# A gated MLP and a linear attention on one core: operands of the spatial products at equal addresses modulo 256

## The chip, the cores and the metric

The kernel runs on one core of a Trainium2 chip. The core has TensorE (PE), VectorE (DVE), ScalarE (ACT), GpSimd (POOL) and SyncE (SP), an on-chip memory of 128 partitions, and accumulators (PSUM) that TensorE writes. A matmul takes a left operand, which is loaded as weights (the profile's PEld), and a right operand, which streams past them. An *address* below is the byte offset of an operand in its partition. The metric is the time of one execution in device microseconds, the median of some runs.

## The reference

Two branches work on a layer-normed x and are added to it: a linear attention with learned features (A), and a gated MLP (B). The change is in the spatial product of B, where a 2048 x 2048 matrix multiplies 2048 x 688 activations:

```python
xn = _layernorm(x, axis=-1)                       # x: 1 x 2048 x 512
z = _gelu(jnp.einsum("bsd,df->bsf", x, w_in))     # here x is xn, F = 1376
z1 = z[..., :Fh]                                  # Fh = 688
z2 = _layernorm(z[..., Fh:], axis=-1)
g = jnp.einsum("ts,bsf->btf", w_sp, z2) + b_sp[None, :, None]
return jnp.einsum("bsf,fd->bsd", z1 * g, w_out)
...
return x + _A_ref(xn, ...) + _B_ref(xn, ...)
```

## The kernel before

All matrix products run in three matmuls each (`mm3`, L55): a number is split into a rounded high part and a rest (`b_parts`, L592: ACT rounds, DVE subtracts), and high x high, high x rest and rest x high are summed in PSUM (L57, L58, L59). `mm3(dst, a, b)` has the left operand in `a` and the right one in `b`.

The program has four stages. First (to about 195 us) come the projections of branch A, tile `proj`, 512 columns wide, with the first half of z (`zps` from `w1`, 344 wide). Then (to 276 us) come the rest of that and the second half of z (`zps` from `w2`), which the loop at L738 norms; `b_split` (L707) makes right operands out of it. Then (276 to 487 us) come the spatial products, tile `g`, and last the output projections (`pout`, 512 wide; `pend`, 256 wide).

The spatial product is done in 2 x 2 blocks with seven products in place of eight. `FORM` (L776) lists them in the order in which they run: P1 = A11 B11, P2 = A12 B21, P6 = S2 T2, P5 = S1 T1, P7 = S3 T3, P3 = S4 B22, P4 = A22 T4. A *step* n (of 32) takes one row pair i and one quarter q of the sum over s; `products` (L790) runs the seven products in it, each for two tiles k of the sum, each in three matmuls: 42 matmuls of 128x344, and 1344 in all. Steps are numbered from 0 here; steps 8 and 9 are the first two quarters of row pair 2. `prep_a` (L606) makes the left operands of step n+2 while step n+1 runs, from blocks of `wst` that SP loads; `drain` and `gate` follow at the end of a row pair.

The order of instructions on each engine is that in which the code issues them, or, where the scheduler that records the program sees room, another: the first seven steps of `g` come out interleaved, the later ones in the order of FORM.

What sets an operand's address:

- A right operand's tile (`b_tile`, L694) has SL = 1408 floats, 5632 bytes or 22 x 256, and is cut to `[2][2][352]`: high and rest lie 2816 bytes apart (11 x 256), and the two halves 1408 bytes, which is 5 x 256 + 128. So the second half has an address that is 128 more modulo 256 than the first. That is called its *class*. `b_split` puts B22, T1 and T2 into first halves, B21, T3 and T4 into second halves, and B11 into the half n % 2.
- A left operand's tile (L613) holds high and rest of one or two operands, each of 256 floats, 1024 bytes. All of them have the same address modulo 256.
- Small tiles named `pad` (L93, L544) and `gap` (L550) shift what comes behind them. In the program as built all left operands of `g` lie at 192 modulo 256, and right operands at 192 (first half) or 64 (second half). Half of the 1344 matmuls of `g` have operands with equal addresses modulo 256, and half have them 128 apart. In `proj`, `zps` and `pout` they are equal.

`zproj` (L138) makes the two column halves of z2 in the order (0, 1) for even s and (1, 0) for odd s, so that `z[:, 1:3]` and `z[:, 0:2]` in `b_split` are the operands of a subtraction.

Of the kernel before, what the change touches and what calls it, by code (L numbers as in the profile page):

```python
# [18 lines left out]
P = 128  # L19
# [22 lines left out]
def mixer(ctx: ExitStack, tc: tile.TileContext, x, x_t, wv, wqkT, phi_bd, wo, w_in, wst, b_r, w_out, out):  # L42
# [47 lines left out]
    bias = cst.tile([P, NT], F32, name="bias")  # L90
    mv_x = cst.tile([P, NT, 2], F32, name="mv_x")
    r_x = cst.tile([P, NT], F32, name="r_x")
    cst.tile([P, 8], F32, name="pad")  # L93

    def rstd_of(mv, r, stats=None):
        if stats is not None:
# [38 lines left out]
    ctx_z = psum("za", 2)  # L135
    za = ctx_z.__enter__()

    def zproj(ps, s, w, order=(0, 1), wide=False):  # L138

        if ps in (za, kv_ps_p):  # L140
            p = [ps.tile([P, D], F32, tag="z", name="zps") for _ in range(2)]
        else:
            q = ps.tile([P, 2, D], F32, tag="z", name="zps")
            p = [q[:, k] for k in range(2)]
        t = xT[s]
        if wide:
            parts = [(slice(0, 2), slice(LW, FC)), (slice(0, 2), slice(0, LW))]
            dst = [p[k][:, :2 * (f.stop - f.start)].rearrange("p (a b) -> p a b", a=2) for k, (_, f) in enumerate(parts)]
            for (_, f), d in zip(parts, dst):
                for c in range(ND):  # L150
                    cs = slice(c * P, (c + 1) * P)
                    zproj.last = mm3(d, (t[:, 0, cs], t[:, 1, cs]), [v[:, :, c, f] for v in w.both], c == 0, c == ND - 1)
            return list(zip(parts, dst))
        for k, j in enumerate(order):
            for c in range(ND):
                cs = slice(c * P, (c + 1) * P)
                zproj.last = mm3(p[k][:, :FC], (t[:, 0, cs], t[:, 1, cs]), (w[j][0][:, c], w[j][1][:, c]), c == 0, c == ND - 1)
        if ps in (za, kv_ps_p):
            return [((slice(k, k + 1),), p[k][:, :FC].unsqueeze(1)) for k in range(2)]
        return [((slice(0, 2),), q[:, :, :FC])]  # L160
# [380 lines left out]

    mid.enter_context(right("pad", 1)).tile([P, P + 8], F32, name="pad")  # L544
    ws = mid.enter_context(right("ws", 1))
    ctx_zw, ctx_w2 = right("zw", 1), right("w2", 1)
    zw = ctx_zw.__enter__()
    w2_pool = ctx_w2.__enter__()
    w2 = Weights(w2_pool, "w2")
    w2_pool.tile([P, QP // 2], F32, name="gap")  # L550
    zbp_ctx = psum("zb", 1)
    zbp = zbp_ctx.__enter__()

# [38 lines left out]
    def b_parts(h, l, src):  # L592
        rounded = round_h(act, h, src)
        rest_l(l, src, h)
        return rounded

    def load_a(n):
        i, q = SEQ[n]
        f = []
        for k in range(2):  # L600
            t = ws.tile([P, QC, P], F32, tag=f"f{k}", bufs=2, name="wf")
            sp.dma_start(t, wst[2 * i + k, :, q * QC:(q + 1) * QC, :])
            f.append(t.rearrange("p (k two) t -> p two k t", two=2))
        return f

    def prep_a(n, f):  # L606

        a, b = f
        pl = hl[n % 2]
        ops = {}  # L610

        def parts(names, src):
            t = pl.tile([P, 2, len(names), 2, P], F32R, tag="".join(names), name="A")  # L613
            prep_a.last = b_parts(t[:, 0], t[:, 1], src)
            for k, m in enumerate(names):
                ops[m] = t[:, 0, k], t[:, 1, k]

        sums = (sm[0].tile([P, 4, 2, P], F32, name="S") if sm else
                zw.tile([P, 4, FC], F32, tag=("T", "z2")[n], bufs=n + 1, name="S").rearrange("p a b -> p (a b)")[:, :8 * P].rearrange("p (a k b) -> p a k b", a=4, k=2))
        parts(("A11", "A12"), a)  # L620
        dve.tensor_tensor(sums[:, 0], b[:, 0], b[:, 1], op=ALU.add)
        dve.tensor_tensor(sums[:, 1], sums[:, 0], a[:, 0], op=ALU.subtract)  # L622
        parts(("S1", "S2"), sums[:, 0:2])
        dve.tensor_tensor(sums[:, 2], a[:, 0], b[:, 0], op=ALU.subtract)
        dve.tensor_tensor(sums[:, 3], a[:, 1], sums[:, 1], op=ALU.subtract)
        parts(("S3", "S4"), sums[:, 2:4])
        parts(("A22",), b[:, 1:2])
        return ops
# [73 lines left out]
            t = x3[0].tile([P, SL], F32R, tag="b", name="B")  # L702
        return t.rearrange("p (a b c) -> p a b c", a=2, b=2)[..., :FC]

    B, b11 = [], None

    def b_split(z, n):  # L707
        nonlocal b11
        tt = zw.tile([P, 4, FC], F32, tag="T", name="T")
        dve.tensor_tensor(tt[:, 0:2], z[:, 1:3], z[:, 0:2], op=ALU.subtract)  # L710
        if n % 2 == 0:
            b11 = b_tile()
        b_parts(b11[:, 0, n % 2], b11[:, 1, n % 2], z[:, 0])
        dve.tensor_tensor(tt[:, 2], z[:, 2], tt[:, 0], op=ALU.subtract)
        ops = {"B11": (b11[:, 0, n % 2], b11[:, 1, n % 2])}
        t = b_tile()
        b_parts(t[:, 0], t[:, 1], z[:, 2:4])
        ops["B22"], ops["B21"] = [(t[:, 0, k], t[:, 1, k]) for k in range(2)]
        dve.tensor_tensor(tt[:, 3], z[:, 3], tt[:, 2], op=ALU.subtract)
        t = b_tile()  # L720
        b_parts(t[:, 0], t[:, 1], tt[:, 0:2])
        ops["T1"], ops["T3"] = [(t[:, 0, k], t[:, 1, k]) for k in range(2)]
# [13 lines left out]

    late, seeds = [], []
    for s in range(NT):  # L738
        p = zproj((kv_ps_p, zc, zbp, za)[s % 4], s, w2, (0, 1) if s % 2 == 0 else (1, 0), s == 0)
        if s < NT - 1:  # L740
            with tc.issue_after(early):
                seeds.append(sp.dma_start(out[s * P:(s + 1) * P, :], x[s * P:(s + 1) * P, :]).ins)
# [20 lines left out]
    ctx_w2.__exit__(None, None, None)  # L763
    x3.append(mid.enter_context(ctx_x3))
    hl[1] = mid.enter_context(left("hl1", 1))
    A[1] = prep_a(1, raw.pop(1))
    raw[2] = load_a(2)
    normed(*late.pop(), ins)
# [377 lines left out]
```

## Time and profile before

| | us |
|---|---|
| median of 3 runs (lowest, highest) | 616.11 (614.33, 617.33) |
| the profiled execution, its own time | 615.49 |
| span of the profiled execution | 613.7 |
| granted TensorE clock, mean | 0.998 |
| first matmul of `g` starts | 276.12 |
| last work on `g` in the window of that tile | before 487.4 |

The profile is one execution. Busy time of an engine is the time that its instructions cover; PE's overlap, so that their durations can't be added up. How far apart matmuls start is read from the timeline, or from the count in a window.

### The profile page before, as it was taken

The numbers are of one execution on the slowest core, as the hardware profiler recorded it, in microseconds if no ns is written. First come the engines' busy times: TensorE is split into PE (matmuls) and PEld (weight loads), VectorE is DVE, ScalarE is ACT, GpSimd is POOL, SyncE is SP. The second block draws the span as 40 slices with busy tenths as digits, with TensorE's granted clock in tenths as the row PEclk, the third lists the DMA queues.
The fourth block names the chain that finished last, engine by engine and source line by source line (L and its number), as shares of the span: only waits on it lengthen the run. The fifth ranks groups of instructions, "written<-read, shape, count | busy, mean of one in ns | idle before, by whom it ended". The sixth has DMA issues, their size and how long they took to land.

```text
span 613.7 us, 11396 instructions
## 1 busy us (share of the span) xinstructions
PE 606.0 (99%) x4286; PEld 551.0 (90%) x4286; DVE 518.8 (85%) x929; ACT 261.1 (43%) x416; POOL 134.7 (22%) x236
## 2 busy tenths in 40 slices
PE   8999999999999999999999999999999999999996
PEld 6888888888888999999999999999999977777775
DVE  5999999999988578899889897877879999999921
ACT  4653324423433547887434443342345343332221
POOL 4122232333111014552000002000100042243520
PEclk9999999999999999999999999999999999999999
DMA  9557876566537849001454646455566799898882
GB/s 310 195 128 178 219 173 186 150 161 171 137 113 210 273 159 321 5 1 35 149 128 141 186 97 184 135 156 148 166 172 206 230 342 328 280 278 238 204 212 59
DMA packets 58414, 109.95 MB, mean 179 GB/s; under 512 B 12456, under 2 KB 24616, under 8 KB 58120
## 3 DMA queue, kind: packets, MB, share of 16 engines
q1 hardware_dynamic: 43400, 64.96, 34.9%
q0 software_dynamic: 12656, 38.64, 24.9%
q10 hardware_dynamic: 2304, 5.64, 2.4%
q8 instruction: 33, 0.54, 0.4%
q14 instruction: 21, 0.17, 0.1%
HBM read 66.85 MB, written 35.80 MB: 167 GB/s over the span
## 4 chain that ended last, share of the span: by engine, by line
PE 85%; DVE 6%; DMA 5%; issue 2%; SPq 1%; ACT 1%; POOL 0%; ACTq 0%; DVEq 0%; POOLq 0%
PE g L57 9%; PE g L58 9%; PE g L59 9%; PE proj L57 7%; PE proj L58 7%; PE proj L59 7%; PE zps L58 6%; PE zps L57 6%; PE zps L59 6%; PE pout L57 4%; PE pout L59 4%; PE pout L58 4%; DMA zacc<-e 1%; PE kvps L373 1%; PE po L1016 1%
## 5 line engine op out<-in xcount | busy, mean ns | idle before, releaser
L57 PE MATMUL g<-B,A 128*128 128x344 f32 x448 | 142.5, 319 | 0.4 <-DVE c L810 0.4
L58 PE MATMUL g<-B,A 128*128 128x344 f32 x448 | 142.3, 319 | 0.0
L59 PE MATMUL g<-B,A 128*128 128x344 f32 x448 | 138.9, 318 | 0.0
L57 PEld LDWEIGHTS g<-B,A 128*128 128x128 f32 x448 | 84.0, 188 | 1.0 <-DVE c L810 0.7
L58 PEld LDWEIGHTS g<-B,A 128*128 128x128 f32 x448 | 84.0, 188 | 0.0
L59 PEld LDWEIGHTS g<-B,A 128*128 128x128 f32 x448 | 83.6, 188 | 0.0
L49 ACT ACTIVATE A<-S 128x512 fp32r<-128x512 f32 x64 | 39.3, 628 | 71.2 <-DVE S L622 47.1
L57 PE MATMUL proj<-wqk_h,xT 128*128 128x512 f32 x128 | 50.1, 391 | 0.0
L59 PE MATMUL proj<-wqk_h,xT 128*128 128x512 f32 x128 | 49.8, 389 | 0.0
L58 PE MATMUL proj<-wqk_l,xT 128*128 128x512 f32 x128 | 49.8, 389 | 0.0
L125 ACT ACTIVATE e<-e,r_x 128x1024 f32<-128x1024 f32 x26 | 29.8, 1149 | 42.3 <-DVE e L124 41.3
L53 DVE TENSOR_TENSOR A<-S,A 128x512 fp32r<-128x512 f32 x64 | 43.0, 687 | 3.0 <-ACT A L49 2.8
L49 ACT ACTIVATE A<-wf 128x512 fp32r<-128x512 f32 (+1 forms) x64 | 32.8, 515 | 27.4 <-DMA wf<-in_wst 17.5
L57 PE MATMUL zps<-w1h,xT 128*128 128x344 f32 (+2 forms) x128 | 40.8, 320 | 0.0
L58 PE MATMUL zps<-w1l,xT 128*128 128x344 f32 (+2 forms) x128 | 40.7, 318 | 0.0
L59 PE MATMUL zps<-w1h,xT 128*128 128x344 f32 (+2 forms) x128 | 40.7, 318 | 0.0
L57 PE MATMUL zps<-w2h,xT 128*128 128x344 f32 (+2 forms) x128 | 40.7, 318 | 0.0
L58 PE MATMUL zps<-w2l,xT 128*128 128x344 f32 (+2 forms) x128 | 40.6, 317 | 0.0
L59 PE MATMUL zps<-w2h,xT 128*128 128x344 f32 (+2 forms) x128 | 40.3, 317 | 0.0
L53 DVE TENSOR_TENSOR A<-wf,A 128x512 fp32r<-128x512 f32 (+1 forms) x64 | 35.1, 553 | 3.9 <-ACT A L49 3.7
L128 DVE TENSOR_REDUCE sm<-e 128x64 f32<-128x1024 f32 x26 | 31.1, 1200 | 2.5 <-ACT e L125 2.5
L787 POOL DMA_DIRECT2D z1t<-z_d x16 | 8.7, 552 | 108.3 <-DMA wf<-in_wst 71.0
(222 smaller groups left out, 1437.4 us busy)
## 6 DMA issues: line engine op xcount, KB each, us to landing
wf<-in_wst SPq DMA_DIRECT2D x64, 256.0 KB, 3.4
e_d<-e POOLq DMA_DIRECT2D x16, 544.0 KB, 4.6
et<-e_d SPq DMA_DIRECT2D x16, 544.0 KB, 7.2
z_d<-z1f ACTq DMA_DIRECT2D x16, 344.0 KB, 3.1
z1t<-z_d POOLq DMA_DIRECT2D x16, 344.0 KB, 4.8
zacc<-e POOLq DMA_DIRECT2D x10, 512.0 KB, 4.8
u<-u_d SPq DMA_DIRECT2D x15, 320.0 KB, 5.8
xt<-in_x SPq DMA_DIRECT2D x16, 256.0 KB, 4.0
```

The source lines that it names most:

```text
L49: return act.activation(h, src, AF.Copy).ins
L53: return (eng or dve).tensor_tensor(l, src, h.bitcast(F32), op=ALU.subtract).ins
L57: pe.matmul(dst, ah, bh, start=start, stop=False)
L58: pe.matmul(dst, ah, bl, start=False, stop=False)
L59: return pe.matmul(dst, al, bh, start=False, stop=stop).ins
L125: softmax_pair.last = less, act.activation(e, e, AF.Exp, scale=scale).ins
L128: dve.tensor_reduce(sm, heads(e), axis=AX.X, op=ALU.add)
L373: i = pe.matmul(kv_acc[k:k + QP, m // 4], vs[:, m * QP:(m + 1) * QP], e[:, m * HP:(m + 1) * HP], start=first and m < 4 and len(ready) == n ...
L787: pool.dma_start(t[:, k, :FH], z1_d[2 * i + k])
L1016: lasts[3] = pe.matmul(po[r][c * QP:(c + 1) * QP, k], kvT[rows, m // 2, cols], fs[m // 4][rows, m // 2 % 2], start=True, stop=True).ins
```

## The change

Right operands: `b_split` now puts B21, T1 and T2 into first halves and B22, T3 and T4 into second halves. B11 of the two tiles k of a quarter q lies in two tiles, one for each k, and in the half q % 2 of them. `zproj` loses its order of columns, and the subtractions take other columns in its place.

Left operands: the four tiles of a step are taken in the order S3 S4, A22, A11 A12, S1 S2. The tile of A11 and A12 is 128 bytes longer; A12 lies 128 bytes later in it, and A11 too where q is even. High and rest of one operand stand side by side (`spread` makes the view), so that ACT and DVE write two pieces of 256 floats where they wrote 512. Pads and gaps get other sizes, and the 8-float pad among the constants goes.

In the program as built, the two operands of each matmul of `g` have equal addresses modulo 256: 160 and 160, or 32 and 32. The order of FORM is as it was, and in it the class alternates. In a step with even q it is one for P1, P2, P6, P5 and the other for P7, P3, P4; with odd q it is the other for P1, the one for P2, P6, P5, the other again for P7, P3, P4. At 86 of the 1344 matmuls the left operand of the matmul that follows has the other class than the right operand of this one. All other tiles but a few constants lie 32 bytes lower modulo 256 than before; `proj`, `zps` and `pout` keep equal addresses, at 160 in place of 192.

Three places in the program's order, with the numbers of the tiles. PE, the first product (P1) of step 8, before; `g` is its accumulator, B and A the operands' tiles:

```order
L57 MATMUL g_3855<-B_2595,A_3752 128x344
L58 MATMUL g_3855<-B_2595,A_3752 128x344
L59 MATMUL g_3855<-B_2595,A_3752 128x344
L57 MATMUL g_3855<-B_2595,A_3752 128x344
L58 MATMUL g_3855<-B_2595,A_3752 128x344
L59 MATMUL g_3855<-B_2595,A_3752 128x344
```

and now:

```order
L57 MATMUL g_3855<-B_2594,A_3753 128x344
L58 MATMUL g_3855<-B_2594,A_3753 128x344
L59 MATMUL g_3855<-B_2594,A_3753 128x344
L57 MATMUL g_3855<-B_2691,A_3753 128x344
L58 MATMUL g_3855<-B_2691,A_3753 128x344
L59 MATMUL g_3855<-B_2691,A_3753 128x344
```

The two k of B11 lay in the two halves of one tile (B_2595), and lie in the same half of two tiles (B_2594, B_2691).

PE, the end of P5 and the start of P7 in the same step, before:

```order
L57 MATMUL g_3876<-B_2699,A_3757 128x344
L58 MATMUL g_3876<-B_2699,A_3757 128x344
L59 MATMUL g_3876<-B_2699,A_3757 128x344
L57 MATMUL g_3883<-B_2603,A_3762 128x344
L58 MATMUL g_3883<-B_2603,A_3762 128x344
L59 MATMUL g_3883<-B_2603,A_3762 128x344
```

and now:

```order
L57 MATMUL g_3876<-B_2699,A_3754 128x344
L58 MATMUL g_3876<-B_2699,A_3754 128x344
L59 MATMUL g_3876<-B_2699,A_3754 128x344
L57 MATMUL g_3883<-B_2602,A_3751 128x344
L58 MATMUL g_3883<-B_2602,A_3751 128x344
L59 MATMUL g_3883<-B_2602,A_3751 128x344
```

No instruction moves. What moves is the tile of S3 and S4 (A_3762, now A_3751): it lay at the class of all left tiles and lies 128 bytes off that of S1 and S2 now, as its right operand does.

ACT, the roundings in the second pair of `b_split`, among those of z2, before:

```order
L733 ACTIVATE z2_2590<-z2_2590,nb_2617,rstd_2613 128x688
L49 ACTIVATE B_2595<-z2_2590 128x344
L49 ACTIVATE B_2606<-T_2593 128x2x344
L748 ACTIVATE z2_2686<-zps_2659,r_x_80 128x344
L748 ACTIVATE z2_2686<-zps_2660,r_x_80 128x344
L733 ACTIVATE z2_2590<-z2_2590,nb_2657,rstd_2653 128x688
L49 ACTIVATE B_2695<-z2_2590 128x2x344
```

and now:

```order
L745 ACTIVATE z2_2589<-z2_2589,nb_2616,rstd_2612 128x688
L49 ACTIVATE B_2605<-T_2592 128x2x344
L760 ACTIVATE z2_2685<-zps_2658,r_x_80 128x344
L760 ACTIVATE z2_2685<-zps_2659,r_x_80 128x344
L49 ACTIVATE B_2691<-z2_2589 128x344
L745 ACTIVATE z2_2589<-z2_2589,nb_2656,rstd_2652 128x688
L760 ACTIVATE z2_2685<-zps_2715,r_x_80 128x688
L49 ACTIVATE B_2695<-z2_2589 128x2x344
```

B11 of the second pair goes to a tile of its own (B_2691) and is rounded three instructions later; it went into the first pair's tile (B_2595). The interleaving of the first seven steps of `g` on PE comes out in another order too.

The diff, without the lines that only pass the dropped argument on:

```diff
-    cst.tile([P, 8], F32, name="pad")
...
-        for k, j in enumerate(order):
+        for k in range(2):
             for c in range(ND):
                 cs = slice(c * P, (c + 1) * P)
-                zproj.last = mm3(p[k][:, :FC], (t[:, 0, cs], t[:, 1, cs]), (w[j][0][:, c], w[j][1][:, c]), c == 0, c == ND - 1)
+                zproj.last = mm3(p[k][:, :FC], (t[:, 0, cs], t[:, 1, cs]), (w[k][0][:, c], w[k][1][:, c]), c == 0, c == ND - 1)
...
-    mid.enter_context(right("pad", 1)).tile([P, P + 8], F32, name="pad")
+    mid.enter_context(right("pad", 1)).tile([P, HP // 4], F32, name="pad")
...
-    w2_pool.tile([P, QP // 2], F32, name="gap")
+    w2_pool.tile([P, QP + HP // 4], F32, name="gap")
...
+    def spread(ap, axis, more):
+        dims = [list(d) for d in ap.ap]
+        dims[axis][0] += more
+        return bass.AP(ap.tensor, ap.offset, dims)
...
+        tiles = {}
+        for names, more in ((("S3", "S4"), 0), (("A22",), 0), (("A11", "A12"), QP), (("S1", "S2"), 0)):
+            tiles[names] = pl.tile([P, D * len(names) + more], F32R, tag="".join(names), name="A")
+
         def parts(names, src):
-            t = pl.tile([P, 2, len(names), 2, P], F32R, tag="".join(names), name="A")
-            prep_a.last = b_parts(t[:, 0], t[:, 1], src)
+            late = QP * (1 - SEQ[n][1] % 2) if "A11" in names else 0
+            more = QP if "A11" in names else 0
+            t = tiles[names][:, late:late + D * len(names)].rearrange("p (m l k t) -> p l m k t", l=2, k=2, t=P)
+            h, l = (spread(t[:, v], 1, more - late) for v in range(2))
+            prep_a.last = b_parts(h, l, src)
             for k, m in enumerate(names):
-                ops[m] = t[:, 0, k], t[:, 1, k]
+                ops[m] = h[:, k], l[:, k]
...
-    B, b11 = [], None
+    B, b11 = [], [None] * 2
...
-        dve.tensor_tensor(tt[:, 0:2], z[:, 1:3], z[:, 0:2], op=ALU.subtract)
-        if n % 2 == 0:
-            b11 = b_tile()
-        b_parts(b11[:, 0, n % 2], b11[:, 1, n % 2], z[:, 0])
-        dve.tensor_tensor(tt[:, 2], z[:, 2], tt[:, 0], op=ALU.subtract)
-        ops = {"B11": (b11[:, 0, n % 2], b11[:, 1, n % 2])}
+        dve.tensor_tensor(tt[:, 0:2], z[:, 1:4:2], z[:, 0:2], op=ALU.subtract)
+        k, q = n % 2, n // 2 % 2
+        if not q:
+            b11[k] = b_tile()
+        b = b11[k][:, 0, q], b11[k][:, 1, q]
+        b_parts(*b, z[:, 0])
+        dve.tensor_tensor(tt[:, 2], z[:, 3], tt[:, 0], op=ALU.subtract)
+        ops = {"B11": b}
         t = b_tile()
         b_parts(t[:, 0], t[:, 1], z[:, 2:4])
-        ops["B22"], ops["B21"] = [(t[:, 0, k], t[:, 1, k]) for k in range(2)]
-        dve.tensor_tensor(tt[:, 3], z[:, 3], tt[:, 2], op=ALU.subtract)
+        ops["B21"], ops["B22"] = [(t[:, 0, k], t[:, 1, k]) for k in range(2)]
+        dve.tensor_tensor(tt[:, 3], z[:, 2], tt[:, 2], op=ALU.subtract)
...
-        p = zproj((kv_ps_p, zc, zbp, za)[s % 4], s, w2, (0, 1) if s % 2 == 0 else (1, 0), s == 0)
+        p = zproj((kv_ps_p, zc, zbp, za)[s % 4], s, w2, wide=s == 0)
...
     hl[1] = mid.enter_context(left("hl1", 1))
+    hl[1].tile([P, QP], F32, name="pad")
```

More of the change, by code (lines that the diff above doesn't have):

```diff
@@ L136, in mixer, with zproj @@
     za = ctx_z.__enter__()
-    def zproj(ps, s, w, order=(0, 1), wide=False):
+    def zproj(ps, s, w, wide=False):
         if ps in (za, kv_ps_p):
@@ L703, in b_tile @@
         return t.rearrange("p (a b c) -> p a b c", a=2, b=2)[..., :FC]
-    B, b11 = [], None
+    B, b11 = [], [None] * 2
     def b_split(z, n):
-        nonlocal b11
         tt = zw.tile([P, 4, FC], F32, tag="T", name="T")
-        dve.tensor_tensor(tt[:, 0:2], z[:, 1:3], z[:, 0:2], op=ALU.subtract)
-        if n % 2 == 0:
-            b11 = b_tile()
-        b_parts(b11[:, 0, n % 2], b11[:, 1, n % 2], z[:, 0])
-        dve.tensor_tensor(tt[:, 2], z[:, 2], tt[:, 0], op=ALU.subtract)
-        ops = {"B11": (b11[:, 0, n % 2], b11[:, 1, n % 2])}
+        dve.tensor_tensor(tt[:, 0:2], z[:, 1:4:2], z[:, 0:2], op=ALU.subtract)
[6 more added lines that the diff above has]
+        ops = {"B11": b}
         t = b_tile()
         b_parts(t[:, 0], t[:, 1], z[:, 2:4])
-        ops["B22"], ops["B21"] = [(t[:, 0, k], t[:, 1, k]) for k in range(2)]
-        dve.tensor_tensor(tt[:, 3], z[:, 3], tt[:, 2], op=ALU.subtract)
+        ops["B21"], ops["B22"] = [(t[:, 0, k], t[:, 1, k]) for k in range(2)]
+        dve.tensor_tensor(tt[:, 3], z[:, 2], tt[:, 2], op=ALU.subtract)
         t = b_tile()
```

## Prediction

> **What bounds the kernel now.** I read the page first, then the waits of PE, then windows and the timeline of PE by stage. From the page, the span, the busy times, the engines' shares of the chain that ended last, and the costliest groups:
>
> ```profile
> span 613.7 us, 11396 instructions
> PE 606.0 (99%) x4286; PEld 551.0 (90%) x4286; DVE 518.8 (85%) x929; ACT 261.1 (43%) x416; POOL 134.7 (22%) x236
> PE 85%; DVE 6%; DMA 5%; issue 2%; SPq 1%; ACT 1%; POOL 0%; ACTq 0%; DVEq 0%; POOLq 0%
> L57 PE MATMUL g<-B,A 128*128 128x344 f32 x448 | 142.5, 319 | 0.4 <-DVE c L810 0.4
> L58 PE MATMUL g<-B,A 128*128 128x344 f32 x448 | 142.3, 319 | 0.0
> L59 PE MATMUL g<-B,A 128*128 128x344 f32 x448 | 138.9, 318 | 0.0
> ```
>
> TensorE is the chain (85%), and the 3 x 448 = 1344 matmuls on `g`, the spatial products that the change touches, wait for nothing but 0.4 us. So no wait is to be won here. What is left is the rate at which one matmul follows another, and a mean of 319 ns doesn't show it, because matmuls overlap. Windows do. Each row has the window, its length, and then busy time and count for PE, PEld, DVE, ACT and POOL, the granted clock, the DMA share and GB/s:
>
> ```profile
> 206.00:212.00 6.00, 6.00 (x40) 6.00 (x40) 2.76 (x7) 3.52 (x9) 0.00 (x0) 1.00 0.96 289
> 222.00:274.00 52.00, 52.00 (x341) 52.00 (x341) 45.84 (x96) 39.54 (x59) 25.00 (x41) 1.00 0.29 101
> 329.00:434.00 105.00, 105.00 (x674) 105.00 (x673) 86.56 (x183) 40.94 (x73) 8.72 (x16) 1.00 0.52 147
> ```
>
> A count holds two matmuls more than start inside, since one lasts 0.32 us and the next starts after half of that. All three windows hold 128x344 matmuls at a granted clock of 1.00. The second (`zps`) makes 339 in 52.00 us, 153.4 ns each; the third, 16 whole steps of `g`, 672 in 105.00 us, 156.25 ns; the first (`zps` again) 38 in 6.00 us, 157.9 ns. The same shape has a fast and a slow rate, and `g` lies between them.
>
> **Where the two rates come from.** The timeline of PE at the ends of blocks in two neighbouring steps (start, length, instruction):
>
> ```profile
> 330.87 0.32 PE L57 MATMUL g<-B,A 128*128 128x344 f32 x1
> ...
> 332.76 0.32 PE L57 MATMUL g<-B,A 128*128 128x344 f32 x1
> ...
> 337.47 0.32 PE L57 MATMUL g<-B,A 128*128 128x344 f32 x1
> ...
> 339.31 0.32 PE L57 MATMUL g<-B,A 128*128 128x344 f32 x1
> ...
> 340.26 0.32 PE L57 MATMUL g<-B,A 128*128 128x344 f32 x1
> ```
>
> The first two rows bound the twelve matmuls of P6 and P5 in step 8, whose operands agree modulo 256: 1.89 us, 157.5 ns each. The next two bound the same twelve in step 9: 1.84 us, 153.3 ns. The six between 339.31 and 340.26 (P7, whose operands are 128 bytes apart) take 0.95 us, 158.3 ns. So operands 128 apart are always slow, but operands that agree are fast or slow by what went before, and they hold their rate through the block. In `zps`, where all operands agree, the slow rate held from 205.02 to 212.44, 47 matmuls at 157.9 ns, and the fast one through the window of 52 us:
>
> ```profile
> 205.02 0.32 PE L57 MATMUL zps<-w1h,xT 128*128 128x344 f32 x1
> ...
> 212.44 0.32 PE L59 MATMUL zps<-w1h,xT 128*128 128x344 f32 x1
> ```
>
> Which operands meet? The weight loads say it:
>
> ```profile
> 337.47 0.19 PEld L58 LDWEIGHTS g<-B,A 128*128 128x128 f32 x1
> ```
>
> The load for the L58 matmul starts when the L57 matmul ahead of it starts (337.47 in both views). What streams together is the right operand of one matmul and the left operand of the *next*. Inside a block the two have equal classes, so that makes no difference; at a seam between classes it does. The earlier steps, which the scheduler interleaves, have single mismatched matmuls in a matched surrounding. Three of them, with rows ahead and behind: the first matmul of the row at 306.88, the one at 321.31, and the second of the row at 324.90.
>
> ```profile
> 306.26 0.32 PE L57 MATMUL g<-B,A 128*128 128x344 f32 x1
> ...
> 306.72 0.32 PE L58 MATMUL g<-B,A 128*128 128x344 f32 x1
> 306.88 0.48 PE L59 MATMUL g<-B,A 128*128 128x344 f32 x2
> 307.20 0.32 PE L57 MATMUL g<-B,A 128*128 128x344 f32 x1
> ...
> 308.30 0.32 PE L57 MATMUL g<-B,A 128*128 128x344 f32 x1
> ...
> 321.31 0.32 PE L57 MATMUL g<-B,A 128*128 128x344 f32 x1
> 321.47 0.32 PE L59 MATMUL g<-B,A 128*128 128x344 f32 x1
> ...
> 322.57 0.32 PE L59 MATMUL g<-B,A 128*128 128x344 f32 x1
> ...
> 324.29 0.32 PE L59 MATMUL g<-B,A 128*128 128x344 f32 x1
> ...
> 324.90 0.47 PE L58 MATMUL g<-B,A 128*128 128x344 f32 x2
> ...
> 325.38 0.32 PE L57 MATMUL g<-B,A 128*128 128x344 f32 x1
> ...
> 326.48 0.32 PE L57 MATMUL g<-B,A 128*128 128x344 f32 x1
> ```
>
> Ahead of the first, three matmuls take 0.46 us (153 ns), ahead of the last, four take 0.61 (153 ns). Behind each of the three, seven matched matmuls take 1.10 us (157 ns). The one at 321.31 was met in the slow rate and left it slow. So one mismatched interval throws the fast rate over into the slow one, and the slow one outlives it.
>
> [...]
>
> **The change, part by part.**
>
> *Own pairs.* Before, half of the 1344 matmuls read operands 128 apart; after, none. If the rate went by a matmul's own pair alone, all of `g` would run as `zps` does from 222 to 274: 1344 x (156.25 - 153.3) = 4.0 us less.
>
> *Seams.* The classes still alternate in the order of FORM, which isn't changed. In an even step P1, P2, P6, P5 (24 matmuls) stand in the right operands' first half and P7, P3, P4 (18) in the second; in an odd step P1 stands in the second, P2, P6, P5 in the first, P7, P3, P4 in the second. That makes four seams in two steps, with 18 or 24 matmuls between them. At each the right operand still streaming has one class and the left operand being loaded has the other: one mismatched interval, as in the three places above. From the fast rate it leads to the slow one; from the slow rate the single one at 321.31 didn't lead back (what did, just ahead of 337.47, was a block of nine). So I expect the first seam, 24 matmuls into the stage, to throw `g` into the slow rate, and the next ones to keep it there: 1344 x (157.9 - 156.25) = 2.2 us more. The seam interval itself costs 5 ns or so, 0.4 us if all 86 did; in the slow rate it replaces an interval nearly as long, and I put it at nothing.
>
> *Operand work.* Left operands are now written as two pieces of 256 where it was one of 512. No row has such a write. The bounds are nothing and the price of two writes of half the size:
>
> ```profile
> L53 DVE TENSOR_TENSOR A<-S,A 128x512 fp32r<-128x512 f32 x32 | 21.5, 687 | 1.7 <-ACT A L49 1.6
> L53 DVE TENSOR_TENSOR A<-wf,A 128x256 fp32r<-128x256 f32 x16 | 6.6, 414 | 0.0
> ```
>
> That is 2 x 414 - 687 = 141 ns on each of three writes, 0.42 us in a step at most. DVE has (105.00 - 86.56) / 16 = 1.15 us idle in a step, by the window above, and PE waits for it only at the end of row pairs. I take nothing; with DVE's cover gone it would be 32 x 0.42 = 13 us, which needs DVE to be the bound, and it stays 0.7 us short of that. The column order in `zproj` and the subtractions in `b_split` have as many elements as before, and lie under the window from 222 to 274, where PE never pauses. The right operands still take 28 tiles in all; a tile for B11 is taken at another pair.
>
> *Addresses elsewhere.* Without the 8-float pad nearly every tile begins 32 bytes lower modulo 256, on the left side of the memory and on the right, so that `proj`, `zps` and `pout` keep operands that agree. All of their operands began at a multiple of 64 before, and none does after. No row shows such a matmul. The low bound is nothing, and the nearest rows for a price are the steady rates of other widths, 512 and 256:
>
> ```profile
> 113.12 0.39 PE L57 MATMUL proj<-wqk_h,xT 128*128 128x512 f32 x1
> ...
> 114.48 0.39 PE L57 MATMUL proj<-wqk_h,xT 128*128 128x512 f32 x1
> ...
> 607.51 0.28 PE L57 MATMUL pend<-woh,oT 128*128 128x256 f32 x1
> ...
> 608.47 0.28 PE L59 MATMUL pend<-woh,oT 128*128 128x256 f32 x1
> ```
>
> Six of 512 take 1.36 us (226.7 ns), eight of 256 take 0.96 us (120 ns). With 153.3 these are 34, 18 and 23 times 6.67 ns, as if operands went in blocks of 64 bytes (512 floats are 32 blocks, 256 are 16). I take nothing, the more likely end, as 32 bytes is a shift of both operands alike; the other end is below.
>
> **The sum.** The profiled execution took 615.49 us. Plus 2.2 is 617.7. It lies 0.6 below the median of 616.11, from which the sum would be 618.3; I predict 618.0. PE is busy up to the end of the stage and behind it (the page's chain), so what `g` loses or wins reaches the end.
>
> **Rivals.**
>
> *B, own pairs decide, or a seam doesn't throw the rate over:* all fast, 4.0 us less, 611.5 to 612.1. For it: matched blocks do run at 153.3, and the seam here moves both operands at once, while in the three places above only the right one moved and came back. Against it: what streams together, by the weight loads' starts. Chance 0.33.
>
> *C, the rates don't follow the pair in the way read here,* or fast and slow blocks alternate as now: 615 to 616.5. For it: equal pairs run at both rates already, so that the change may do what it says and still buy nothing. Against it: `zps` holds one rate for 52 us. Chance 0.12.
>
> *D, slower: the shift by 32 bytes.* If the 64-byte blocks are real, a 512-wide operand now touches 33 of them instead of 32, and each such matmul takes one step of 6.67 ns more:
>
> ```profile
> 0.00:613.70 613.70, 136.84 (x576) 106.90 (x576) 79.78 (x128) 11.03 (x16) 1.00 0.63 179
> 0.00:613.70 613.70, 106.88 (x452) 83.83 (x452) 0.69 (x1) 8.98 (x15) 1.00 0.63 179
> ```
>
> These windows count the matmuls of `proj` (576) and `pout` (452): 1028 x 6.67 = 6.9 us, so 623 to 625. A 344-wide one (21.5 blocks) touches 22 either way. It decides if the interval in `proj` reads 233 ns instead of 227. Chance 0.15.
>
> **How the numbers follow.** My case (A, `g` locked in the slow rate) has 0.40; its own range is 617.0 to 619.2. B has 0.33, C 0.12, D 0.15. Cases of both signs are likely, so the range takes in A, B and C, from 611.3 to 620.6, and leaves out D and the edges, 2 in 10. About 0.5% (613.0 to 619.2) is what a measurement of this kernel can tell from no change. Faster than that is B without its upper edge, 0.31; slower is D and A's upper edge, 0.18; the rest, 0.51, is within.
>
> **What would show it.** Right: windows inside `g` with 316 or 317 starts in 50 us (now 320), and the timeline's first 24 products of the stage at 153 ns, the next at 158. B: 326 starts in 50 us throughout. D: six `proj` matmuls in 1.40 us instead of 1.36. A wait of PE for DVE or ACT inside `g` that is longer than the 0.4 us now would make the part on operand work wrong.

## The result, and the profile after

| | before | after |
|---|---|---|
| median (lowest, highest), us | 616.09 (614.33, 617.33), 4 runs | 624.16 (622.58, 627.06), 4 runs |
| ratio, with its 95% interval | | 1.0139 [1.0093, 1.0184] |
| the profiled execution, its own time | 615.49 | 623.54 |

The change made the kernel 1.4% slower, by 8.05 us in the profiled executions. From the page of the changed kernel, the span, the shares of the chain, and the groups on `g`:

```profile
span 621.8 us, 11389 instructions
...
PE 77%; DVE 8%; POOL 4%; ACT 4%; issue 3%; DMA 3%; SPq 0%; ACTq 0%; POOLq 0%; DVEq 0%
...
L57 PE MATMUL g<-B,A 128*128 128x344 f32 x448 | 142.6, 319 | 2.0 <-ACT A L49 1.1
L58 PE MATMUL g<-B,A 128*128 128x344 f32 x448 | 142.3, 319 | 0.5 <-DVE B L53 0.5
L59 PE MATMUL g<-B,A 128*128 128x344 f32 x448 | 138.5, 318 | 0.2 <-DVE A L53 0.2
```

The busy time of `g` is what it was, 423.4 us on the three lines against 423.7 before, with 318 or 319 ns for one matmul in both (these durations overlap and don't show the rate), and TensorE now waits inside `g`. Waits of PE from the start of that stage on, in total, times and longest (`A` and `B` are the operands of `g`, `c` is what `drain` makes of it):

```profile
PE pout L57 <- DVE c L823: 4.3, 1, 4.3
PE g L57 <- ACT A L49: 1.1, 1, 1.1
PE g L57 <- DVE c L823: 0.9, 2, 0.4
PE g L58 <- DVE B L53: 0.5, 1, 0.5
PE g L59 <- DVE A L53: 0.2, 1, 0.2
```

The rate itself is fast. The windows of the prediction, on the changed kernel (PE, PEld, DVE, ACT, POOL; clock; DMA):

```profile
222.00:274.00 52.00, 52.00 (x342) 52.00 (x341) 45.26 (x94) 38.84 (x58) 24.75 (x39) 1.00 0.28 99
329.00:434.00 105.00, 105.00 (x687) 105.00 (x686) 86.53 (x182) 41.01 (x72) 8.72 (x16) 1.00 0.52 146
```

685 starts in 105 us are 153.3 ns each, as in `zps`; before it was 672, 156.25 ns. So the loss is elsewhere, and two windows hold most of it, here first after, then before:

```profile
285.00:300.00 15.00, 13.26 (x72) 12.19 (x71) 13.28 (x27) 7.05 (x14) 1.19 (x2) 0.90 0.38 119
480.00:500.00 20.00, 15.68 (x84) 13.80 (x90) 15.83 (x27) 6.45 (x12) 3.17 (x6) 0.83 0.79 228
```

```profile
285.00:300.00 15.00, 15.00 (x97) 14.74 (x96) 13.42 (x27) 6.72 (x12) 1.19 (x2) 1.00 0.42 133
480.00:500.00 20.00, 20.00 (x130) 16.92 (x129) 19.34 (x33) 6.30 (x10) 4.58 (x8) 1.00 0.83 260
```

At 285 to 300, the second to fourth step, TensorE stands still for 1.74 us and then runs at a lower clock (granted 0.90 in this window, 1.00 before); at 480 to 500, where `g` hands over to `pout`, it loses 4.32 us and clock again (0.83, 1.00 before). The most useful view for all that follows is the *lag*: the start of the n-th matmul on a tile in PE's timeline, less the start of the n-th before the change. (The first eight steps of `g` come out interleaved, not seven, and not in one order in all kernels, so that up to there the two need not be the same matmul.) It adds up to the 8.0 us at the end: -0.44 at the first `g`, 3.77 lost up to step 4, 1.78 won back up to the last `g`, 4.35 lost up to the first `pout`, 2.10 lost inside `pout`.

```
lag, us          first g  step 4  step 15  last g  first pout  50th pout  last pout | median, us (before beside it)
after             -0.44    3.33    2.08    1.55      5.90        8.29       8.00    | 624.16 (616.09)
e1                -0.33    1.87    1.61    0.29      3.47        6.58       6.94    | 624.79 (615.36)
e2                 0.32    0.19   -0.26   -0.89     -0.66       -0.67      -0.18    | 614.36 (615.36)
e3                -0.79    2.34    1.10    1.06      2.74        8.05       7.62    | 624.27 (615.36)
e4                -0.34   -0.63   -1.79   -1.76     -1.74       -1.73      -1.45    | 615.59 (615.36)
e5                -0.28    2.08    0.83    0.86      0.94        2.14       4.09    | 620.67 (616.48)
e6                 0.36    0.33   -0.92    0.11      4.10        5.69       5.70    | 621.90 (616.48)
e7                 0.15    0.63    0.19   -1.57     -0.63       -0.63      -0.40    | 615.75 (616.48)
e8                 0.03    0.15   -1.10   -0.41      0.64        0.64       2.48    | 615.86 (616.48)
e9                -0.04    0.11   -1.13   -0.23      0.37        1.35       2.44    | 617.48 (615.80)
e10               -0.19   -0.32   -0.77   -2.07     -2.21        0.16      -0.30    | 616.46 (615.80)
e11               -0.37   -0.46   -1.71   -3.83     -3.97       -1.58      -2.03    | 616.20 (615.80)
e12               -0.29    0.68    0.68   -0.11     -0.24        2.13       1.69    | 618.30 (615.80)
e13               -0.10    0.85   -0.40   -2.53     -2.66       -1.51      11.81    | 627.68 (616.20)
e14               -0.18   -0.19   -0.19   -0.98     -1.11        0.04      16.14    | 630.79 (616.20)
e15                0.19    0.06   -0.39   -2.14     -2.28       -1.14      14.38    | 629.50 (616.20)
e16               -0.68   -0.11   -1.36   -4.10     -4.23        1.35       8.99    | 624.63 (615.74)
e17                0.33    0.33    0.33   -0.46     -0.59        7.70      14.63    | 625.93 (615.74)
e18               -0.39   -0.52   -0.97   -2.73     -2.86        3.71      10.87    | 624.77 (615.74)
```

A row is one profiled execution, and the median is over several; e1's row comes from its fastest one (622.42), e8's and e17's from slow ones of theirs (618.35 and 630.28). Step 4 and step 15 are the first matmuls of these steps, and `pout` is counted from 0.

### The profile page after: what moved, and what is told of

Read it like the earlier page. It is cut to its first block, busy times and chain, and to the rows that moved or that the text cites. A ratio compares the mean times of both kernels' runs of the same rounds, so it can differ in the third digit from the quotient of the medians.

```text
span 621.8 us, 11389 instructions
## 1 busy us (share of the span) xinstructions
PE 607.6 (98%) x4286; PEld 551.0 (89%) x4286; DVE 520.4 (84%) x929; ACT 261.3 (42%) x416; POOL 135.5 (22%) x236
## 4 chain that ended last, share of the span: by engine, by line
PE 77%; DVE 8%; POOL 4%; ACT 4%; issue 3%; DMA 3%; SPq 0%; ACTq 0%; POOLq 0%; DVEq 0%
PE g L57 8%; PE g L58 8%; PE g L59 8%; PE proj L58 7%; PE proj L57 7%; PE proj L59 7%; PE pout L57 6%; PE pout L59 5%; PE pout L58 5%; PE zps L59 3%; PE zps L58 3%; PE zps L57 3%; DVE A L53 1%; POOL rstd L98 1%; PE po L1029 1%
```

## The experiments

### The grouping alone, and all but the grouping (e1, e2)

e1 is the kernel before with only this:

```diff
+        k, q = n % 2, n // 2 % 2
+        if not q:
+            b11[k] = b_tile()
+        b = b11[k][:, 0, q], b11[k][:, 1, q]
```

> The kernel before, with one thing of the change: the tile for B11 is shared by pairs n and n+2 instead of n and n+1. Addresses and left operands stay as before, so that half of the matmuls on `g` still read operands 128 bytes apart. Theory G (the grouping of B11 makes both new waits: by the order it gives ACT and DVE around 275 to 294 us, and by the slot that two of the three `wof` tiles then share): the waits appear here too, about 2 us of them at 285 to 300 and about 4 on `c` ahead of `pout`, with low-clock matmuls behind each, and no gain of rate: 622 to 627 us. Theory L (the waits come from the left operands' new writes and tiles, or from TensorE reaching its operands earlier at the faster rate): no new wait here, 615 to 617.5.

e2 is the changed kernel with those lines as before (`if n % 2 == 0: b11 = b_tile()`).

> The changed kernel, with B11 grouped as before (pairs n and n+1 share a tile); all else as changed. 1248 of the 1344 matmuls on `g` read operands that agree, 96 (half of P1) are 128 bytes apart. Theory G: the order on every engine is that of before, so neither wait is there; the rate is fast but for some 175 single intervals of 4 to 5 ns more, 0.8 us: 616.1 - 4.0 + 0.8 = 612.9, say 612.2 to 613.8. Theory L: the waits stay, 619 to 624. If single mismatched intervals threw the rate over for good, as the prediction had it: 616 to 618.5 with windows of 322 or fewer in 50 us. If the shift by 32 bytes cost anything outside `g`, 1 to 7 us more than theory G's time.

e1 took 624.79 us against 615.36, ratio 1.0148 [1.0114, 1.0182], and e2 614.36, ratio 0.9982 [0.9965, 0.9998]. In the lag, e1 has both losses and e2 neither. The waits of PE in e1 are those of the change:

```profile
PE pout L57 <- DVE c L811: 3.2, 1, 3.2
PE pout L57 <- ACT oT L49: 1.4, 1, 1.4
PE g L57 <- ACT A L49: 1.1, 1, 1.1
PE g L58 <- DVE B L53: 0.4, 1, 0.4
```

So theory G holds: which pairs share a tile for B11 costs all of it, and the left operands, the new addresses and the 32 bytes cost nothing that shows in e2. e2 came out 0.6 over its range. Its rate is half-way (677 starts, 155.1 ns):

```profile
329.00:434.00 105.00, 105.00 (x679) 105.00 (x679) 86.50 (x183) 40.94 (x73) 8.72 (x16) 1.00 0.51 147
```

Its intervals say why. Each block of three mismatched matmuls in P1 that was met in the fast rate was followed by the slow one (22 of 22, from step 7 on and away from waits), which lasted to a seam.

### The late loss: one slot (e3, e5)

e3 is the changed kernel with

```diff
-        t = [xz2.tile([P, SL], F32, tag="b", name="wof") for _ in range(3)]
+        t = [xz2.tile([P, SL], F32, tag="b", name="wof") for _ in range(2)]
+        t = [t[c // 2][:, c % 2 * D:(c % 2 + 1) * D] if c < 4 else
+             ws.tile([P, QC, P], F32, tag=f"f{c % 2}", bufs=2, name="wof").rearrange("p a b -> p (a b)") for c in range(KF + 1)]
```

> The changed kernel, with the last three loads of the output weights (`wof`) in the small tiles of `wf`, which are free by then, instead of a third tile of the right operands' pool. Theory G: the early waits stay, the wait of 4.3 us on `c` ahead of `pout` and the low clock behind it go: 624.2 - 4.3 - 1 to 2 = 617.5 to 619.5. If the shared slot isn't what makes the drain late: 623 to 625.

It took 624.27, ratio 1.0148 [1.0111, 1.0184]: nothing won. The wait on `c` shrank from 4.3 to 1.7, and another one stands behind it:

```profile
PE pout L57 <- ACT oT L49: 3.4, 1, 3.4
PE pout L57 <- DVE c L823: 1.7, 1, 1.7
```

Here `oT`, which ACT rounds, is an operand of the output stage. SP's queue has the reason. `kvT` is a load for the attention of that stage, and the loads of the attention's weights (`wof` from `in_wo`, which go out from 489.48 on in the changed kernel and from 481.42 on before) stand in the queue behind it. Before, after, and e3 (start, length, instruction):

```profile
480.99 0.38 SPq L980 DMA_DIRECT2D kvT<-kvT_d  x1
```

```profile
469.33 8.75 SPq L863 DMA_DIRECT2D wof<-in_w_out  x7
...
489.05 0.33 SPq L993 DMA_DIRECT2D kvT<-kvT_d  x1
```

```profile
468.87 6.86 SPq L863 DMA_DIRECT2D wof<-in_w_out  x7
...
488.56 0.33 SPq L995 DMA_DIRECT2D kvT<-kvT_d  x1
```

In the built programs `kvT` lies over the right-operand slot at 152512 (152480 now). Before, that slot held a tile of pair 2 or 3, last read in step 28. Pairs 0 and 1 now take eight tiles instead of seven, their eighth lands there, and their quarter is the last one of the last row pair (`SEQ`): it is read to the end of `g`. The third `wof` tile lost its own slot in the same way and shares another one. e5 swaps the two tiles:

```diff
-        if k < 10:
+        if k < 11 and k != 7:
```

> The changed kernel with two right-operand tiles swapped between pools: the eighth, which belongs to pair 1 and is read until the last step, goes where the eleventh stood, and the eleventh, of pair 2, which is done three steps earlier, takes its place at address 152480. Theory S (one slot: in the change this address is read until the end of the stage, and both the third `wof` tile and the `kvT` load ahead of the attention weights stand in line for it): the late loss, 4.3 us up to the first `pout` matmul and 2.4 us behind it, goes, and the early 3.3 us stay: 617.5 to 619.5. Rival (the late loss comes from the recorded order, or from anything else that moved with the grouping): 623 to 625.

620.67, ratio 1.0063 [1.0045, 1.0082]; 4.2 us over before, where the change was 8.1 over. The 4.35 us up to the first `pout` are 0.08. `kvT` goes out 5.5 us earlier:

```profile
468.66 4.75 SPq L863 DMA_DIRECT2D wof<-in_w_out  x7
...
479.61 2.71 SPq L938 DMA_DIRECT2D f<-q_d  x4
483.55 0.38 SPq L993 DMA_DIRECT2D kvT<-kvT_d  x1
```

Theory S holds for the hand-over, but 3.2 us are lost inside `pout`, where 2.4 were expected to go too, and the median is 1.2 over the range. SP stands for 3 us ahead of `f` here (its load before ends at 476.6). The built programs and the traces say what it stands for. The swap gives pair 1's eighth tile, which is read to the end of `g`, a slot of the pool that `f` comes from, so that the tiles behind it take slots that come free later. The first of `f`'s two slots is read for the last time by the 1266th matmul on `g` before, and `f` goes out 0.03 us after that one's end (475.28); in e5 it is the 1287th, and `f` goes out 0.03 us after its end (479.58). In the changed kernel `f`'s slots are read last by the same matmuls as before, so this cost is the swap's own and not one of the change. That it makes up all of the 3.2 us isn't shown.

### The early loss: the order on ACT and DVE (e6, e9)

The order rows ahead of the prediction show B11 of the second pair on ACT behind the last T of the first. Busy time up to 285 us, before, after and in e1:

```profile
205.00:285.00 80.00, 80.00 (x518) 79.44 (x517) 67.00 (x138) 58.77 (x94) 29.16 (x49) 1.00 0.39 132
```

```profile
205.00:285.00 80.00, 80.00 (x520) 79.47 (x519) 65.04 (x133) 56.86 (x91) 29.45 (x48) 1.00 0.38 131
```

```profile
205.00:285.00 80.00, 80.00 (x520) 79.48 (x519) 64.94 (x133) 56.75 (x91) 29.51 (x48) 1.00 0.38 131
```

By then DVE and ACT have each done 2 us less of the same work. The waits that grew in this stretch are DVE's for ACT's `z` (from 0.7 to 3.1 us, while those for `B` shrank from 4.8 to 3.0) and ACT's for `nb`, which GpSimd makes (from 9.9 to 12.9). A few us later TensorE wants what is missing. The last rounding on ACT that it waits for, before and after:

```profile
291.15 0.78 ACT L49 ACTIVATE B<-T 128x688 fp32r<-128x688 f32 x1 [1.19 <-DVE T L719]
```

```profile
293.48 0.78 ACT L49 ACTIVATE B<-T 128x688 fp32r<-128x688 f32 x1 [1.19 <-DVE T L731]
```

e6 leaves the grouping and mends the order: the second B11 tile is made with the first, and something small is written to its unused columns, so that B11 of the second pair isn't the first write of a new tile.

```diff
+        if touch:
+            pool.memset(t[:, SL - 8:].bitcast(F32), 0.0)
...
-        if not q:
-            b11[k] = b_tile()
+        if n % 4 == 0:
+            b11[:] = b_tile(), b_tile(touch=True)
```

> The changed kernel, with the second B11 tile made at pair 0 together with the first and touched by a small write of GpSimd in its unused columns, so that the write of B11 of pair 1 is no longer the first one of a new tile; on ACT's queue it then stands ahead of the last T of pair 0, as before the change. Theory O (the early waits come from the order in which ACT and DVE prepare the right operands): the lag at the 120th matmul on `g`, 1.8 us, and the 3.3 us at the 168th shrink below 1, the late loss stays: 620.5 to 622. Rival (the early waits come from the tiles themselves, whatever the order): 623 to 625.

621.90, ratio 1.0079 [1.0054, 1.0105]; the lag stays at 0.3 up to step 4, and DVE and ACT are back at their old work:

```profile
205.00:285.00 80.00, 79.95 (x517) 79.39 (x518) 67.07 (x137) 58.69 (x94) 28.46 (x51) 1.00 0.38 132
```

Theory O holds. The late loss is still there (5.6 us from the last `g` to the end). e9 has both mends:

> The changed kernel with both mends together: the touched B11 tile of the sixth experiment and the swapped tiles of the fifth; addresses and grouping as in the change. If the two losses are separate and have the two causes found (the order on ACT and DVE at 285 to 300, one slot at 152480 at the end), the lag has neither the 3.8 us early nor the 4.3 us at the first `pout` matmul; some of the 3.2 us that the fifth still lost inside `pout` may stay: 616.5 - 1 to + 2.5, 615.5 to 619. If one mend undoes the other, or there is a third cost in the grouping: 620 to 623.

617.48, ratio 1.0032 [1.0012, 1.0052]: of 8.1 us 1.7 are left. The lag has neither loss; 2.1 us go inside `pout`, as in e5. The two causes are separate, and they make up at least four fifths of the loss; what is left lies where the swap makes `f` late (here too it goes out 3 us later than before, at 478.52).

### All pairs matched without the grouping, and what becomes of the rate (e4, e7, e8)

e4 is e2 with A11 in a tile of its own, so that its two k can have two classes as B11 has them; P1 runs its second k first.

```diff
-        parts(("A11", "A12"), a)
+        parts(("A11",), a[:, 0:1])
+        parts(("A12",), a[:, 1:2])
...
+                h, l = (bass.AP(t.tensor, t[:, v * P:].offset, [list(t.ap[0]), [D, 1], [2 * P + QP, 2], [1, P]]) for v in range(2))
```

> The changed kernel with B11 grouped as before, and A11 in a tile of its own, its second block 128 bytes on, so that all 1344 matmuls on `g` read operands that agree; within P1 the second block goes first, so that a step has two seams as in the changed kernel. ACT and DVE get one more instruction in each step (two of 128x256 for one of 128x512, 0.15 to 0.2 us). Theory G: no wait, all fast but for the seams: 616.1 - 4.0 + 0.4 = 612.5, say 611.5 to 613.0. If the added instructions make TensorE wait at the ends of row pairs: 613 to 616. Theory L: 619 or more.

615.59, ratio 1.0003 [0.9983, 1.0022]: 2.6 over the range. The lag wins 1.45 up to step 15 and then nothing. What eats it, as the waits have it, is DVE at the ends of row pairs:

```profile
PE g L57 <- DVE c L820: 0.9, 2, 0.4
```

TensorE comes earlier to the accumulators that `drain` frees, and DVE has preparation of left operands queued ahead of it. The wait costs more than it reads: at step 16 the lag loses 1.02 us, where the wait reads 0.4. It is counted from the end of the matmul ahead, 0.32 us after that one's start. Six matmuls there start 203 to 753 ns after the one ahead, together 1.07 us more than at 153 ns each; the slow rate, which holds behind them up to a seam, adds 0.1. The one wait in the kernel before, 0.4 us at step 28, costs 0.8 in the same way. e7 (on e2) and e8 (on e4) put that preparation behind the start of the drain:

```diff
+            with ExitStack() as held:
+                if n % NQ == NQ - 1:
+                    held.enter_context(tc.issue_after(cb[1]))
+                    held.enter_context(tc.issue_after(drain.second))
+                A[n + 2] = prep_a(n + 2, raw.pop(n + 2))
```

> The kernel of the second experiment (changed addresses, B11 grouped as before) with one rule more: at the end of a row pair, the left operands of two steps on are prepared behind the first two operations of the drain (the copy of P1 on ACT, the sum with P2 on DVE). Theory R (the rate won on `g` is lost again where TensorE, now early, waits for the drain of the pair before, and in the slow stretch behind such a wait): the losses at steps 24 and 28, 0.5 and 0.3 us, go, 613.2 to 614.2. Rival (DVE has no room, a drain served first makes the left operands late): 614.5 to 617.

> The kernel of the fourth experiment (all pairs matched, A11 apart) with the same rule for the drain. There the lag shows losses at steps 10, 16, 20 and 24 of 0.3, 1.0, 0.7 and 0.2 us, where DVE's `c` is waited for. Theory R: most of that goes, 615.6 - 1.9 = 613.7, say 612.5 to 614.5. Rival: 615 to 617.5.

615.75, ratio 0.9981 [0.9959, 1.0004], and 615.86, ratio 0.9986 [0.9966, 1.0007]. In e7's trace the losses at steps 24 and 28 are gone, as theory R has it (-0.38 at step 25, -1.41 at step 29), and 0.94 of it is given back at the first `pout`, which waits for the last drain. e8's trace, of an execution 2.5 us over its median, still has waits from step 20 on. Both medians miss the range of theory R and lie in the rival's. For e7 that is the number and not the mechanism, since no matmul on `g` waits in its trace from step 7 on. The gain, 0.6 to 0.7 us, is no more than the intervals leave open.

### The hand-over (e10 to e18)

Three more kernels have that rule and move the features of the third row tile (`q_fin`, 4.8 us of DVE) behind the last drain. e10 is made from e2, e11 from e4, and e12, the control, from the kernel before, with its addresses:

```diff
+    with tc.issue_after(cb[2]):
+        es[2], last = q_fin(ets.pop(2), qtmp, zb)
```

> The kernel of the seventh experiment (changed addresses, B11 grouped as before, drain first), with the features of the third row tile taken behind the last drain on DVE instead of ahead of it. There the lag was -1.6 us at the end of the stage and -0.6 at the first `pout` matmul, which waited 0.9 for `c`. If the rate won is given back only at that hand-over, it now reaches the end: 1.2 to 2 us under before. If `pout` is bound by DVE and the DMA queues anyway (92 and 98% busy there), it is lost later in the stage: 0 to 0.7 us under before.

> The same two rules on the kernel of the fourth experiment (all pairs matched): by the first theory 1.5 to 3 us under before, by the second 0 to 1.

> Control: the kernel before, addresses and all, with the two rules (drain first, features behind the last drain). TensorE doesn't come early there and waits 0.4 us in all, so the rules alone should buy nothing: within 0.5 us of before, by either theory. What the tenth and eleventh gain over this one is what the addresses bring.

616.46 (1.0011 [0.9990, 1.0032]), 616.20 (1.0000 [0.9980, 1.0020]) and 618.30 (1.0030 [1.0005, 1.0054]). Neither theory has these times: e10 and e11 were to be 0 to 3 us under before, and e12 within 0.5. e11 wins 3.46 us from the first to the last `g`, with 684 starts in 105 us. Not all of that is the rate: 0.7 is won at step 28 in e12 as well, where before loses its 0.8. e12 on the whole loses 0.18, since it has waits of its own in steps 2 and 3. But the rule costs each of the three 2.4 us up to the 50th `pout`. PE's wait there in e11, which e10 and e12 have too (`ul` is the rest of an operand of `pout`):

```profile
PE pout L59 <- DVE ul L53: 2.2, 1, 2.2
```

e13 to e15 put the features behind `ul`, and also the attention's rounding of `oT` behind the last split of `wof`; e16 to e18 are e10 to e12 with all of the features but their first product behind `ul`; in each set the first has e4's addresses, one is the control with those of before, and one has e2's.

> The kernel of the eleventh experiment (all pairs matched, B11 grouped as before, drain first), with the features of the third row tile one place further back on DVE: behind the `ul` that the eleventh waited 2.2 us for. Theory R (the rate won on `g`, 3.5 us in the eleventh's trace at the end of the stage, is real, and only what DVE serves first at the hand-over decides how much of it reaches the end): the wait goes, 3 to 4 us under before in the trace and 2.5 to 3.5 in the median. Rival (`pout` is bound by DVE and the DMA queues, a wait taken away there comes back further on): 0 to 1.5 us under before.

> Control: the kernel before with the same rules on DVE and ACT and with its own addresses. The wait of 2.2 us that the rules brought in the twelfth goes: within 1 us of before by either theory. By theory R it is 3 to 4 us over the thirteenth, by the rival not over 1.5.

> The kernel of the tenth experiment (1248 of 1344 matched, fast for about half of the time) with the features behind `ul`. Theory R: half of what the thirteenth gains, 1.5 to 2.5 us under before. Rival: 0 to 1.5.

> The kernel of the eleventh experiment with one thing moved: of the features of the third row tile, all behind their first product stands behind `ul` on DVE, so that the loads of `et` keep nearly their place on SP's queue, which the thirteenth put them off by 6 us. Theory R (the 3.5 us won on `g` reach the end where nothing that TensorE needs at the hand-over is late): without the eleventh's wait of 2.2 us on `ul`, 2 to 4 us under before. Rival (`pout` takes it back at the next wait, for `oT` or for the features): 0 to 1.5 us under before.

> Control: the kernel before with the same rules and its own addresses: by theory R 2.5 to 4 us over the sixteenth, about before's time; by the rival within 1.5 us of the sixteenth.

> The same rules on the kernel of the second experiment (half of the rate gain): by theory R 1 to 2 us under before, half-way between the sixteenth and the seventeenth; by the rival all three within 1.5 us.

All six lost 9 to 15 us, and the wait on `ul` came back as others, here in e13 and e16:

```profile
PE po L1033 <- DMA f<-q_d: 4.7, 1, 4.7
PE ptq L1016 <- DVE et L570: 3.2, 1, 3.2
```

```profile
PE po L1034 <- DMA f<-q_d: 6.1, 1, 6.1
PE pout L58 <- DVE wol L53: 2.6, 1, 2.6
```

Both theories fail for the absolute times: features that come later are missed further on. The comparison inside a set is left. All pairs matched against the addresses of before, under one rule: 616.20 against 618.30, 627.68 against 630.79, 624.63 against 625.93, so 2.1, 3.1 and 1.3 us, where `g` in the traces won 3.6, 1.6 and 2.6 more than in the control. With half of the rate (e10, e15, e18) it is 1.8, 1.3 and 1.2. By what was expected, the 3.1 is theory R's and the 1.3 the rival's. All six differences have one sign. Drawing the runs again at random puts the three with all pairs matched at 0.8 to 4.1, 0.2 to 4.4 and 0.4 to 3.9 us (95%, rough for so few runs); of the three with half of the rate, only e10's (0.4 to 2.7) doesn't reach zero. So the rate gain is real, and some of it reaches the end. None of the 18 kernels beats before clearly; the nearest is e2, 0.2% with an interval that ends at 0.9998.

## Why the prediction was wrong

618.0 us were forecast in 611.3 to 620.6; 624.16 came. Two of its steps failed, with opposite signs.

**"Operand work", the last sentence.** "The right operands still take 28 tiles in all; a tile for B11 is taken at another pair" was costed at nothing, and the opening part said that no wait was to be won, which isn't that none could be made. This is the step that failed, a cost put at nothing: the regrouping alone costs 9.4 us (e1), and without it the changed kernel is 9.1 us faster against before (e2, 1.0 under where the change is 8.1 over). Two things that were in sight weren't priced. The order rows showed B11 of the second pair three instructions later on ACT, in a stretch in which DVE is busy for 67 of 80 us. And 28 tiles in all says nothing of how long each of them is read: a quarter that is read last took one tile more, and that tile's slot was spoken for. The prediction named the sign to look for, "A wait of PE for DVE or ACT inside `g` that is longer than the 0.4 us now"; it is there, 1.1 us for ACT.

**"Seams".** "So I expect the first seam, 24 matmuls into the stage, to throw `g` into the slow rate": it doesn't. Step 9 in the changed kernel, its first matmul and that of step 10:

```profile
338.37 0.32 PE L57 MATMUL g<-B,A 128*128 128x344 f32 x1
...
344.82 0.32 PE L57 MATMUL g<-B,A 128*128 128x344 f32 x1
```

6.45 us for 42 matmuls: 39 at 153.3 ns and three seams at 157.5. Of 44 seams met in the fast rate from step 7 on, away from waits, all 44 were followed by the fast rate; in e11 54 of 54. The three places from which the rule was drawn had the right operand alone change its class and come back. The prediction said so, as an argument for its rival, and gave that rival 0.33 against 0.40. So the term of +2.2 us should have been -4.0 + 86 x 4.5 ns = -3.6. On `g`, e11's trace wins 3.5 us, e16's 3.4 and e13's 2.4, of which the rule for the drain gives 0.8 by itself (e14 and e17).

**The rivals.** B was right on the rate (685 starts in 105 us) and wrong on the time, since it took the rest to be nothing, too. D's time, 623 to 625, was hit for a reason that isn't D's: six `proj` matmuls take 1.36 us as before, and the lag at the first `g` is -0.44, where D has 3.8 us for the 576 of `proj`. So nothing here shows its blocks of 64 bytes.

```profile
113.03 0.39 PE L57 MATMUL proj<-wqk_h,xT 128*128 128x512 f32 x1
...
114.39 0.39 PE L57 MATMUL proj<-wqk_h,xT 128*128 128x512 f32 x1
```

**What held.** The two-piece writes cost nothing; the bound of 141 ns was at its low end (687 ns before):

```profile
L53 DVE TENSOR_TENSOR A<-S,A 128x512 fp32r<-128x512 f32 x64 | 42.9, 685 | 3.0 <-ACT A L49 3.0
```

"What `g` loses or wins reaches the end" held only in part: the sets of e10 to e18 show 1.2 to 3.1 us of it there, and e4, e7 and e8 0 to 0.7, since DVE, at the ends of row pairs and at the hand-over, is not ahead by as much as the rate wins.

## What to carry to other kernels

When a change hands buffers out differently, follow each buffer to its last reader and to whoever gets its memory next, above all loads that one engine issues one behind the other: here one slot that was held 3 steps longer kept back every load behind it, and cost 4.3 us up to the first `pout`, more than the rate could win. A mend that moves a buffer hands out slots differently, too (e5). A mend of the wait that the profile names (e3) may only uncover the next one of the same cause, so look for what the waits have in common before mending. And a rate that is to be won on the busiest engine is worth what its neighbours leave of it (2.1 of 3.6 us between e11 and e12): compare kernels that differ in the rate alone, under one and the same order.

## What wasn't expected of the hardware

A matmul of 128x344 with operands equal modulo 256 ran at 153.3 or at 157.5 to 158 ns in these traces, and what went with it is what ran before. From step 7 on, away from waits: blocks of nine mismatched matmuls (before) turned the fast rate into the slow one 13 of 13 times and the slow into the fast one 11 of 11; blocks of three (e2, e7) the fast into the slow one 46 of 46 times; blocks of six (before) left either rate as it was, 47 of 47 times. e1, whose blocks from step 8 on are all even (6 or 18), stayed fast behind 59 of 59, and made 675 starts in the 105 us where before made 672, with as many mismatched matmuls. So in these runs an odd block turned the rate over and an even one didn't; the exceptions stand where steps come interleaved (a block of four in before and e12, one of two in e1, two seams in a row in e4). A seam by itself, at which both operands change, cost 4 to 5 ns and turned nothing over in the fast rate. After a wait the slow rate held up to a seam: in the changed kernel at 157.6 to 158.3 ns up to the first one, 17 matmuls, behind the wait that ended at 466.56, and to the second, 41 matmuls, behind the one that ended at 439.51.

Behind a stall of 1.1 us that ended at 296.89, the clock granted to TensorE was 0.52 from 297 to 300 in the changed kernel, with matmuls 287 ns apart in the timeline; e1 and e5, which have stalls of 1.1 us on the same operand, were granted 1.00 in that window. The changed kernel and e1:

```profile
297.00:300.00 3.00, 3.00 (x11) 3.00 (x12) 2.55 (x7) 0.94 (x3) 0.00 (x0) 0.52 0.69 236
```

```profile
297.00:300.00 3.00, 3.00 (x19) 3.00 (x20) 2.56 (x7) 0.95 (x3) 0.00 (x0) 1.00 0.68 238
```

The number ahead of the last two is the granted clock, 0.52 and 1.00. So a wait had no fixed price here: 1.5 us of the early 3.8 are this clock (the lag goes from 1.81 at the 120th matmul to 3.29 at the 132nd; in e1 it stays at 1.89).
